# Linear attention beside a top-8 gated MLP: the reciprocal denominator spread inside DRAM, late transfers on one queue

## The chip, the cores and the metric

The kernel runs on one core of a Trainium2 chip. The metric is the time of one execution on the device, in microseconds. Five engines work side by side, each through its own list of instructions in order: TensorE (PE in the profile; its weight loads are PEld) multiplies matrices into PSUM, VectorE (DVE) and ScalarE (ACT) work on elements, GpSimd (POOL) does small work and indirect transfers, and SyncE (SP) only issues transfers. Sixteen DMA engines move the data. SyncE and ScalarE each have a queue of their own for the transfers they issue; an engine that waits for something before it issues a transfer holds back all that stands behind it in its list.

## The reference

Input x has 2048 tokens of 640 features. It is normalised (`xn`), and the output is the sum of three things: x itself, linear attention on `xn`, and a branch B on `xn`.

```
x = A_x; xn = layernorm(x)
q, k, v = split(xn @ wqkv)            # 32 heads of 20 features
phi(t) = (t + 1 if t > 0 else exp(t)) + 1e-6
kv = sum_s phi(k)_s (x) v_s;  z = sum_s phi(k)_s
den = phi(q) . z + 1e-6               # one number per token and head
A = ((phi(q) @ kv) / den) @ wo
r = xn @ w_r; idx = the 8 tokens with the largest r
y = (silu(xn[idx] @ w_gate) * (xn[idx] @ w_up)) @ w_down * sigmoid(r[idx])
out = x + A + xn + (y added to rows idx)
```

Data are bfloat16.

## The kernel before, in words

The 2048 tokens are 16 tiles of 128 partitions. First the tiles are normalised and transposed, and for each tile TensorE computes phi(k) and accumulates the Gram matrix of `xn` and phi(k), from which kv is made later. The queries are computed transposed: `pqT` holds phi(q) with features on partitions and tokens along the free axis, in 20 units (`q_mm`, L271; `q_act`, `q_phi`), five units for each block of 512 tokens.

The attention output of one tile is one product, `o_mm` (L778): `pqT` of the tile against `Ms`, which is kv times wo folded into one matrix. For that, phi(q) has to be divided by den beforehand. `den_mm` (L565) puts den into PSUM with four groups of tokens stacked on the partitions: partition 32 j + h holds head h of token group j. `den_act` (L574) makes 1/den of it with a logarithm and an exponential on ScalarE (`rden`). But `pqT` has one partition for each feature, and 20 features share a head, so each row of `rden` has to appear 20 times on other partitions. This goes through DRAM: `rden_out` or `rden_out_b` (L582, L594) writes each row 20 times from SBUF into a DRAM buffer with one row per feature (`rd`, `rd2`, `rd3`), and `rden_in` or `rden_in_b` (L588, L600) reads that into `spare`, on the partitions of `pqT`. `rden_mul` (L603) and `rden_mul_b` (L607) then multiply `pqT` by it on VectorE. It is done in three parts: tokens 0 to 1023 (offset 0, groups of 256), tokens 1024 to 1535 (offset 1024, groups of 128) and tokens 1536 to 2047 (offset 1536, groups of 128). The first part is written by one transfer of ScalarE and read by two of SyncE. The second is written by four transfers of SyncE, the third by four that ScalarE and SyncE issue in turn. Both are read back by SyncE.

Branch B picks the 8 tokens, gathers their columns, computes gate and up (`gate_up`) and `down`, and scales into `y8`. The rows that have to be changed lie in any tile. For the last five tiles (TS = 11) the kernel puts the residual rows into a DRAM copy `s_dram` (`load_s`, L112), GpSimd adds `y8` to it by an indirect transfer (L837), and the rows are read back into `x_sb` (L842). For tiles 0 to 10 another indirect transfer adds `y8` to the output in DRAM after those tiles have been stored (L849).

The last stage is the loop over t (L823): `o_mm(t)` on TensorE, `o_out(t)` (L788) adds the residual rows on VectorE and stores the tile; interleaved are `down`, the third part of 1/den (t = 0), the reload (t = 5), and the multiplies, `rden_mul` at t = 0 and 1, `rden_mul_b(t + 2)` from t = 6 to 13. Output tiles take turns in two groups of four buffers, one group for even and one for odd t. Stores of t = 0, 1, 2, 3 and of odd t are issued by ScalarE, the others by SyncE. `o_last` handles tile 15 in pieces.

The order of the instructions on every engine is the order of the code; nothing rearranges it. A framework adds the waits: for data, for buffers, and for landing counters. There are eight such counters for the transfers of SyncE and ScalarE together, used in turn; a transfer isn't issued before the last one on the same counter has landed.

Of the kernel before, what the change touches and what calls it, by code (L numbers as in the profile page):

```python
# [8 lines left out]
P = 128  # L9
S = 2048  # L10
D = 640
H = 32
DH = D // H
F = 1536
T = S // P
KC = D // P
FC = F // P
# [9 lines left out]
TS = 11  # L27
NS = TS * P

BF16 = mybir.dt.bfloat16  # L30
# [4 lines left out]
ALU = mybir.AluOpType  # L35
# [3 lines left out]
def kernel(  # L39
# [12 lines left out]
    nc = tc.nc  # L52
# [14 lines left out]
        return sm.tile(shape, dtype, tag=name, name=name)  # L67

    ps = psum.tile([P, 8, 512], F32, tag="ps", name="ps")
    rd = tc.dram_tile([4, D, 256], BF16, name="rd")  # L70
    rdb = [tc.dram_tile([D, 512], BF16, name=f"rd{tb}") for tb in (2, 3)]
    s_dram = tc.dram_tile([S - NS, D], BF16, name="s_dram")

    x_sb = big.tile([P, T, D], BF16, tag="x_sb", name="x_sb")
# [55 lines left out]
    def load_wd(lo, hi):  # L130
        SP.dma_start(wd[:, lo:hi, :], B_w_down.rearrange("(fc p) n -> p fc n", p=P)[:, lo:hi, :])
# [376 lines left out]
    load_wo()  # L508
    kcw(wu, B_w_up, 2, 3)
    kcw(wu, B_w_up, 3, KC)  # L510
    for i in range(0, FC, 4):
        load_wd(i, i + 4)
    PE.transpose(psb[0:T, 1, 0:P], r_all[:], ident[:])
    g1(T - 4)
    r_row = sb("r_row", [T, P], F32)
# [63 lines left out]
        return rden  # L579


    def rden_out(rden):  # L582
        A.dma_start(
            rd[:, :, :].rearrange("j (h i) t -> (j h) i t", i=DH),
            rden[:].unsqueeze(1).to_broadcast([P, DH, 256]),
        )

    def rden_in(j):  # L588
        SP.dma_start(
            spr[:, j * KC : (j + 2) * KC, :],  # L590
            rd[j : j + 2, :, :].rearrange("j (m p) t -> p (j m) t", p=P),
        )

    def rden_out_b(eng, i, rden, j):  # L594
        eng.dma_start(  # L595
            rdb[i][:, j * P : (j + 1) * P].rearrange("(h i) t -> h i t", i=DH),
            rden[32 * j : 32 * j + 32, :].unsqueeze(1).to_broadcast([32, DH, P]),
        )

    def rden_in_b(i):  # L600
        SP.dma_start(sprb[i], rdb[i][:, :].rearrange("(m p) t -> p m t", p=P))

    def rden_mul(j):  # L603
        sl = pqT[:, :, j * 256 : (j + 1) * 256]
        V.tensor_tensor(out=sl, in0=sl, in1=spr[:, j * KC : (j + 1) * KC, :], op=ALU.mult)

    def rden_mul_b(t):  # L607
        sl = pqT[:, :, t * P : (t + 1) * P]
        V.tensor_tensor(  # L609
            out=sl, in0=sl, in1=sprb[t // 12][:, :, t % 4 * P : (t % 4 + 1) * P], op=ALU.mult  # L610
        )

    def kv_mm(bs, bank):
# [87 lines left out]
    spr = sp_rows(0, 8, 256)  # L701
    sprb = [sp_rows(8, 12, 512), sp_rows(12, T, 512)]
# [74 lines left out]

    def o_mm(t):  # L778
        b0 = 2 * (t % 2)
# [8 lines left out]
    def o_out(t):  # L788
        b0 = 2 * (t % 2)
        o_t = evk.tile([P, 2, HW], BF16, tag=("ek", "rk")[t % 2], name=f"o{t}")  # L790
        V.tensor_tensor(  # L791
            out=o_t[:], in0=ps[:, b0 : b0 + 2, 0:HW],
            in1=x_sb[:, t, :].rearrange("p (b f) -> p b f", b=2), op=ALU.add,
        )
# [28 lines left out]
    for t in range(T - 1):  # L823
        o_mm(t)
        if t == 0:
            down()
            den_mm(1536, P, 6)
            rden3 = den_act(1536, P, 6)
            for j in range(4):
                rden_out_b((A, SP)[j % 2], 1, rden3, j)  # L830
            rden_in_b(1)
            for i in range(4):
                A.activation(  # L833
                    y8[:, i * QW : (i + 1) * QW], ps[32 * i : 32 * i + C, 5 + 2 * (i % 2), 0:QW],
                    AF.Identity, scale=gate[32 * i : 32 * i + C, 2:3],
                )
            G.indirect_dma_start(  # L837
                s_dram[:, :], bass.IndirectOffsetOnAxis(ap=idx_i[0:C, 1:2], axis=0), y8[:], None,
                bounds_check=S - NS - 1, oob_is_err=False, compute_op=ALU.add,
            )  # L840
        if t == 5:
            A.dma_start(x_sb[:, TS:T, :], s_dram[:, :].rearrange("(t p) d -> p t d", p=P))  # L842
# [39 lines left out]
```

## Time and profile before

| | |
|---|---|
| median of 3 timed runs | 114.94 us (113.46 to 117.36) |
| the profiled execution | 112.75 us |
| its span in the profile | 111.0 us |
| TensorE busy | 104.3 us |
| VectorE busy | 81.2 us |
| ScalarE busy | 58.9 us |
| GpSimd busy | 39.2 us |
| granted TensorE clock | 1.0 |

The span runs from the first to the last instruction of the profiled execution; the rest of its 112.75 us lies around it. Times within the profile are counted from the span's start. The profile shows when an instruction ran on its engine, when a transfer was issued (lines with SPq or ACTq), and, in the groups of transfers, how long it was from issue to landing.

### The profile page before, as it was taken

The numbers are of one execution on the slowest core, as the hardware profiler recorded it, in microseconds if no ns is written. First come the engines' busy times: TensorE is split into PE (matmuls) and PEld (weight loads), VectorE is DVE, ScalarE is ACT, GpSimd is POOL, SyncE is SP. The second block draws the span as 40 slices with busy tenths as digits, with TensorE's granted clock in tenths as the row PEclk, the third lists the DMA queues.
The fourth block names the chain that finished last, engine by engine and source line by source line (L and its number), as shares of the span: only waits on it lengthen the run. The fifth ranks groups of instructions, "written<-read, shape, count | busy, mean of one in ns | idle before, by whom it ended". The sixth has DMA issues, their size and how long they took to land.

```text
span 111.0 us, 2501 instructions
## 1 busy us (share of the span) xinstructions
PE 104.3 (94%) x897; PEld 61.8 (56%) x906; DVE 81.2 (73%) x186; ACT 58.9 (53%) x155; POOL 39.2 (35%) x86
## 2 busy tenths in 40 slices
PE   5899999999999999999999999999999999994990
PEld 2256645555555555564447788534457776662660
DVE  1798997789999996544349745696799766884780
ACT  1449996797877666555058352788894400000000
POOL 6903563211344448899993420000000050000040
PEclk9999999999999999999999999999999999999999
DMA  3999435792679998999999949369868199999243
GB/s 81 324 328 297 152 68 101 197 240 59 183 189 203 210 177 206 224 220 302 235 388 365 304 110 287 98 173 302 292 91 151 51 344 254 242 359 386 89 124 118
DMA packets 31655, 23.65 MB, mean 213 GB/s; under 512 B 14194, under 2 KB 30362, under 8 KB 31642
## 3 DMA queue, kind: packets, MB, share of 16 engines
q1 hardware_dynamic: 25168, 18.97, 64.3%
q10 hardware_dynamic: 6410, 4.51, 13.2%
q8 instruction: 7, 0.11, 0.5%
q14 instruction: 6, 0.05, 0.2%
q0 software_dynamic: 64, 0.01, 0.2%
HBM read 15.44 MB, written 6.08 MB: 194 GB/s over the span
## 4 chain that ended last, share of the span: by engine, by line
PE 73%; DMA 14%; ACT 3%; issue 3%; DVE 2%; ACTq 2%; SPq 0%
PE ps L274 19%; PE ps L237 19%; PE ps L266 16%; PE ps L782 5%; DMA spare<-rd 5%; DMA out_dram<-o 4%; PE ps L502 4%; DMA rd<-rden 3%; DMA x_sb<-in_A_x_dram 2%; PE ps L617 2%; PE ps L634 2%; PE ps L717 2%; PE ps L215 1%; PE ps L808 1%; ACTq L595 1%
## 5 line engine op out<-in xcount | busy, mean ns | idle before, releaser
L237 PE MATMUL ps<-wk,xnT 128*128 128x320 bf16 (+1 forms) x160 | 25.0, 300 | 0.1
L274 PE MATMUL ps<-xnT,wq 128*128 128x512 bf16 x93 | 22.9, 379 | 0.6 <-issue 0.3
L782 PE MATMUL ps<-late,pqT 128*128 128x320 bf16 x150 | 21.6, 299 | 1.4 <-DVE pqT L609 1.4
L237 PEld LDWEIGHTS <-xnT 128*128 128x128 bf16 x160 | 15.1, 98 | 8.7 <-ACT xnT L221 0.9
L266 PE MATMUL ps<-pk,xn 128*128 128x512 bf16 x78 | 19.5, 379 | 0.1
L251 ACT ACTIVATE ek<-ps 128x320 bf16<-128x320 f32 x32 | 14.8, 463 | 8.1 <-PE ps L237 8.1
L782 PEld LDWEIGHTS <-pqT 128*128 128x128 bf16 x150 | 14.1, 98 | 8.7 <-DVE pqT L609 3.1
L283 ACT ACTIVATE eq<-ps 128x512 bf16<-128x512 f32 x20 | 11.9, 597 | 9.0 <-PE ps L274 9.0
L175 DVE BATCH_NORM_STATS2 stats<-x_sb 128x6 f32<-128x320 bf16 x32 | 14.8, 474 | 2.3 <-DMA x_sb<-in_A_x_dram 2.3
L290 DVE SCALAR_TENSOR_TENSOR pqT<-eq,rq 128x512 bf16<-128x512 bf16 x20 | 13.7, 685 | 3.7 <-ACT rq L284 3.7
L259 DVE SCALAR_TENSOR_TENSOR pk<-ek,rk 128x640 bf16<-128x640 bf16 x16 | 13.0, 813 | 4.2 <-ACT rk L252 4.2
L791 DVE TENSOR_TENSOR o<-ps,x_sb 128x640 bf16<-128x640 f32 x15 | 12.3, 823 | 4.7 <-PE ps L782 3.5
L274 PEld LDWEIGHTS <-wq 128*128 128x128 bf16 x100 | 9.3, 98 | 10.7 <-issue 0.7
L252 ACT ACTIVATE rk<-ps 128x320 bf16<-128x320 f32 x32 | 14.8, 463 | 0.0
L207 POOL TENSOR_SCALAR x_sb<-x_sb,rs,nm 128x640 bf16<-128x640 bf16 x13 | 13.8, 1068 | 0.6
L266 PEld LDWEIGHTS <-xn 128*128 128x128 bf16 x80 | 7.7, 98 | 8.1
L284 ACT ACTIVATE rq<-ps 128x512 bf16<-128x512 f32 x20 | 11.9, 593 | 0.0
L186 POOL TENSOR_SCALAR t<-mv 128x1 bf16<-128x1 f32 x12 | 3.8, 316 | 21.7 <-DVE mv L177 21.4
L818 ACT CAST o<-ps 128x160 bf16<-128x160 f32 x1 | 0.3, 292 | 19.1 <-PE ps L808 19.1
L187 POOL TENSOR_TENSOR rs<-t,mhalf 128x1 f32<-128x1 bf16 x12 | 10.0, 834 | 1.0
L837 POOL DMA_INDIRECT s_dram<-y,idx_i x1 | 1.6, 1594 | 23.2 <-ACT y L833 23.2
L196 DVE TENSOR_SCALAR xn<-x_sb,mv,rs 128x640 bf16<-128x640 bf16 x16 | 7.2, 450 | 3.3 <-POOL rs L187 2.8
(123 smaller groups left out, 98.6 us busy)
## 6 DMA issues: line engine op xcount, KB each, us to landing
spare<-rd SPq DMA_DIRECT2D x4, 640.0 KB, 5.4
wg<-in_B_w_gate_dram SPq DMA_DIRECT2D x5, 384.0 KB, 3.4
wd<-in_B_w_down_dram SPq DMA_DIRECT2D x3, 640.0 KB, 13.5
out_dram<-o ACTq DMA_DIRECT2D x9, 160.0 KB, 4.0
rd<-rden ACTq DMA_DIRECT2D x1, 1280.0 KB
wu<-in_B_w_up_dram SPq DMA_DIRECT2D x3, 384.0 KB, 3.5
wo<-in_A_wo_dram SPq DMA_DIRECT2D x2, 500.0 KB, 7.7
x_sb<-in_A_x_dram SPq DMA_DIRECT2D x3, 320.0 KB, 5.8
```

What stands on the lines that cost most here:

```text
L175: V.bn_stats(out=stats[:, t, b, :], in_=x_sb[:, t, b * HW : (b + 1) * HW])
L207: G.tensor_scalar(out=x_sb[:, t, :], in0=x_sb[:, t, :], scalar1=rs1[:, sl], scalar2=nm[:, sl], op0=ALU.mult, op1=ALU.add,)
L237: PE.matmul(ps[:, b0 + b, 0:n], lhsT=xnT[:, kc, t * P : (t + 1) * P], rhs=wk[:, kc, b * HW : b * HW + n], start=(kc == 0), stop=(kc == KC ...
L251: A.activation(e[:, b, :], ps[:, b0 + b, 0:HW], AF.Exp)
L252: A.activation(r[:, b, :], ps[:, b0 + b, 0:HW], AF.Relu)
L259: V.scalar_tensor_tensor(out=pk[:, t, :].rearrange("p (b f) -> p b f", b=2), in0=e[:], scalar=1.0, in1=r[:], op0=ALU.min, op1=ALU.add,)
L266: PE.matmul(ps[:, 2 + c, :], lhsT=xn[:, t, c * P : (c + 1) * P], rhs=pk[:, t, 0:512], start=(t == 0), stop=(t == T - 1),)
L274: PE.matmul(ps[:, bank, :], lhsT=wq[:, kc, m * P : (m + 1) * P], rhs=xnT[:, kc, tb * 512 : (tb + 1) * 512], start=(kc == 0), stop=(kc == K ...
L283: A.activation(e[:], ps[:, bank, :], AF.Exp)
L290: V.scalar_tensor_tensor(out=pqT[:, m, tb * 512 : (tb + 1) * 512], in0=e[:], scalar=1.0, in1=r[:], op0=ALU.min, op1=ALU.add,)
L782: PE.matmul(ps[:, b0 + b, 0:HW], lhsT=pqT[:, kc, t * P : (t + 1) * P], rhs=Ms[:, kc, b * HW : (b + 1) * HW], start=(kc == 0), stop=(kc == ...
L791: V.tensor_tensor(out=o_t[:], in0=ps[:, b0 : b0 + 2, 0:HW], in1=x_sb[:, t, :].rearrange("p (b f) -> p b f", b=2), op=ALU.add,)
```

## The change

The three parts of 1/den take a common form, with the offset as key (`parts` gives the width of a token group):

- Out of SBUF each row goes once, not 20 times: four small transfers for a part, into `rdh`, one row per head.
- A transfer from DRAM to DRAM, `rden_copy`, repeats each row 20 times, into `rds`, one row per feature.
- One transfer reads `rds` into `spare`. For the first part that is one transfer of 1280 KB in place of two of 640 KB.

All of these transfers are issued by SyncE now. Their places in its list: the first part's copy stands where its reads stood, then the store to `s_dram`, then the read; the second part's copy stands behind its four small writes, its read behind query unit 19; the third part's copy stands behind its four small writes at t = 0, its read at t = 3. The stores of output tiles 0 to 5 are all issued by SyncE, and so is the reload of `x_sb` from `s_dram`. ScalarE keeps the stores of tiles 7, 9, 11, 13 and the last piece of tile 15. w_down is loaded in six transfers of two chunks, not three of four. No instruction that computes is added, removed or moved on its engine.

```diff
-    rd = tc.dram_tile([4, D, 256], BF16, name="rd")
-    rdb = [tc.dram_tile([D, 512], BF16, name=f"rd{tb}") for tb in (2, 3)]
+    parts = {0: 256, 1024: P, 1536: P}
+    rdh = {o: tc.dram_tile([H, 4 * w], BF16, name=f"rdh{o}") for o, w in parts.items()}
+    rds = {o: tc.dram_tile([D, 4 * w], BF16, name=f"rds{o}") for o, w in parts.items()}
...
-    for i in range(0, FC, 4):
-        load_wd(i, i + 4)
+    for i in range(0, FC, 2):
+        load_wd(i, i + 2)
...
+    def rden_out(eng, o, rden):
+        w = parts[o]
+        for j in range(4):
+            eng.dma_start(rdh[o][:, j * w : (j + 1) * w], rden[32 * j : 32 * j + 32, :])
+
+    def rden_copy(eng, o):
         eng.dma_start(
-            rdb[i][:, j * P : (j + 1) * P].rearrange("(h i) t -> h i t", i=DH),
-            rden[32 * j : 32 * j + 32, :].unsqueeze(1).to_broadcast([32, DH, P]),
-        )
+            rds[o][:, :].rearrange("(h i) t -> h i t", i=DH),
+            rdh[o][:, :].unsqueeze(1).to_broadcast([H, DH, 4 * parts[o]]),
+        )
+
+    def rden_in(eng, o):
+        eng.dma_start(spr[o], rds[o][:, :].rearrange("(m p) t -> p m t", p=P))
...
-    rden_out(den_act(0, 256, 6))
+    rden0 = den_act(0, 256, 6)
+    rden_out(SP, 0, rden0)
...
-    for j in (0, 2):
-        rden_in(j)
+    rden_copy(SP, 0)
     load_s(TS, T)
+    rden_in(SP, 0)
...
-    for j in range(4):
-        rden_out_b(SP, 0, rden2, j)
+    rden_out(SP, 1024, rden2)
+    rden_copy(SP, 1024)
...
-    rden_in_b(0)
+    rden_in(SP, 1024)
...
-        eng = nc.sync if t % 2 == 0 and t > 2 else nc.scalar
+        eng = nc.sync if t % 2 == 0 or t < 6 else nc.scalar
...
-            for j in range(4):
-                rden_out_b((A, SP)[j % 2], 1, rden3, j)
-            rden_in_b(1)
+            rden_out(SP, 1536, rden3)
+            rden_copy(SP, 1536)
...
+        if t == 3:
+            rden_in(SP, 1536)
         if t == 5:
-            A.dma_start(x_sb[:, TS:T, :], s_dram[:, :].rearrange("(t p) d -> p t d", p=P))
+            SP.dma_start(x_sb[:, TS:T, :], s_dram[:, :].rearrange("(t p) d -> p t d", p=P))
```

More of the change, by code (lines that the diff above doesn't have):

```diff
@@ L579, in den_act @@
         return rden
[L582 to L585, printed above, removed]
[L586 to L601 removed]
+    def rden_out(eng, o, rden):
[3 more added lines that the diff above has]
+    def rden_copy(eng, o):
+        eng.dma_start(
+            rds[o][:, :].rearrange("(h i) t -> h i t", i=DH),
+            rdh[o][:, :].unsqueeze(1).to_broadcast([H, DH, 4 * parts[o]]),
+        )
+    def rden_in(eng, o):
+        eng.dma_start(spr[o], rds[o][:, :].rearrange("(m p) t -> p m t", p=P))
     def rden_mul(j):
         sl = pqT[:, :, j * 256 : (j + 1) * 256]
[L605 removed]
+        V.tensor_tensor(out=sl, in0=sl, in1=spr[0][:, :, j * 256 : (j + 1) * 256], op=ALU.mult)
     def rden_mul_b(t):
@@ L609, in rden_mul_b @@
         V.tensor_tensor(
-            out=sl, in0=sl, in1=sprb[t // 12][:, :, t % 4 * P : (t % 4 + 1) * P], op=ALU.mult
+            out=sl, in0=sl, in1=spr[t // 4 * 512][:, :, t % 4 * P : (t % 4 + 1) * P], op=ALU.mult
         )
@@ L699, in sp_rows @@
         return spare[:, a:b, :].rearrange("p a b -> p (a b)").rearrange("p (r f) -> p r f", f=w)
-    spr = sp_rows(0, 8, 256)
-    sprb = [sp_rows(8, 12, 512), sp_rows(12, T, 512)]
+    spr = {o: sp_rows(o // P, o // P + w // 32, 4 * w) for o, w in parts.items()}
     Ms = late[:, 0:KC, :]
-    for j in (0, 2):
-        rden_in(j)
+    rden_copy(SP, 0)
     load_s(TS, T)
+    rden_in(SP, 0)
     A.copy(GT[:, 0:4, 512:D], ps[:, 2, :].rearrange("p (c f) -> p c f", c=4))
```

## The prediction

> **What bounds the kernel now.** I read the page's head first, then its share of the chain that ended last.
>
> ```profile
> span 111.0 us, 2501 instructions
> PE 104.3 (94%) x897; PEld 61.8 (56%) x906; DVE 81.2 (73%) x186; ACT 58.9 (53%) x155; POOL 39.2 (35%) x86
> ...
> PE 73%; DMA 14%; ACT 3%; issue 3%; DVE 2%; ACTq 2%; SPq 0%
> ```
>
> TensorE is busy for 94% of the span, so a change that touches only transfers can gain little: the gaps that a transfer causes. The table of waits and the chain in order of time show where such a gap is.
>
> ```profile
> PE ps L782 <- DVE pqT L609: 1.4, 1, 1.4
> ```
>
> ```profile
> 86.71 0.74 ACTq L595
> ...
> 88.33 4.73 DMA out_dram<-o
> 93.06 0.02 issue
> 93.08 3.19 DMA rd<-rden
> ...
> 96.33 5.34 DMA spare<-rd
> 101.66 0.02 issue
> 101.69 0.50 DVE pqT L609
> 102.19 0.05 issue
> 102.24 2.89 PE ps L782 x20
> ...
> 108.15 0.29 ACT o L818
> ```
>
> The last quarter hangs on 1/den of tokens 1536 to 2047 (block 3): written to DRAM, read back into `spare` at 101.66, multiplied into `pqT` by VectorE, used by TensorE at 102.24. The output store of 88.33 stands in this chain although its data have nothing to do with 1/den. In the program every DMA takes one of eight landing counters in turn, and an issue waits until the DMA eight places before it has landed; the fourth write of 1/den stood eight behind that store. TensorE idles 1.4 us, once. That is the most that the change can win inside the span.
>
> VectorE sets when each thing is needed. Columns: start, duration, engine, line, operation, tiles, and in brackets idle time and its releaser.
>
> ```profile
> 81.00 0.82 DVE L605 TENSOR_TENSOR pqT<-pqT,spare 128x1280 bf16<-128x1280 bf16 x1
> ...
> 94.31 0.48 DVE L609 TENSOR_TENSOR pqT<-pqT,spare 128x640 bf16<-128x640 bf16 x1
> 95.09 0.82 DVE L791 TENSOR_TENSOR o<-ps,x_sb 128x640 bf16<-128x640 f32 x1 [0.29 <-PE ps L782]
> ...
> 96.48 0.83 DVE L791 TENSOR_TENSOR o<-ps,x_sb 128x640 bf16<-128x640 f32 x1 [0.17 <-issue]
> ...
> 99.39 0.82 DVE L791 TENSOR_TENSOR o<-ps,x_sb 128x640 bf16<-128x640 f32 x1 [0.17 <-issue]
> 101.69 0.49 DVE L609 TENSOR_TENSOR pqT<-pqT,spare 128x640 bf16<-128x640 bf16 x1 [1.48 <-DMA spare<-rd]
> 102.10 0.82 DVE L791 TENSOR_TENSOR o<-ps,x_sb 128x640 bf16<-128x640 f32 x1
> 102.83 0.48 DVE L609 TENSOR_TENSOR pqT<-pqT,spare 128x640 bf16<-128x640 bf16 x1
> ```
>
> So the first part of 1/den is due at 81.0, block 2 at 94.3, block 3 at 100.2 (end of the output add of 99.39, token tile 10). The add of tile 8 (96.48) reuses the buffer of tile 0, so tile 0 must have been stored by then. The add of tile 11 (102.10) needs the rows of `x_sb` that are reloaded from `s_dram`.
>
> **The change part by part.** The times at which 1/den is ready, and the issues of SyncE now (first start, sum of the group):
>
> ```profile
> 63.91 0.42 ACT L578 ACTIVATE rden<-ld 128x256 bf16<-128x256 f32 x1
> ...
> 79.91 0.31 ACT L578 ACTIVATE rden<-ld 128x128 bf16<-128x128 f32 x1
> ...
> 85.71 0.31 ACT L578 ACTIVATE rden<-ld 128x128 bf16<-128x128 f32 x1
> ...
> 87.50 0.38 ACT L833 ACTIVATE y<-ps,gate 8x160 bf16<-8x160 f32 x1 [1.48 <-issue]
> ...
> 93.63 0.39 ACTq L842 DMA_DIRECT2D x_sb<-s_dram  x1
> ```
>
> ```profile
> 49.55 5.97 SPq L131 DMA_DIRECT2D wd<-in_B_w_down_dram  x3
> 71.75 1.16 SPq L589 DMA_DIRECT2D spare<-rd  x2
> 73.02 1.79 SPq L113 DMA_DIRECT2D s_dram<-x_sb  x1
> 80.24 3.16 SPq L595 DMA_DIRECT2D rd<-rden  x4
> 86.12 0.37 SPq L601 DMA_DIRECT2D spare<-rd  x1
> ```
>
> Prices of transfers come from landings (issue to landing: writes of L595, 160 KB each; reads into `spare`, 640 KB; the reload; the smallest store) and from what the DMA engines moved in three stretches (last number, GB/s): reads in 512-byte pieces, writes in 256-byte pieces, long pieces.
>
> ```profile
> DMA to landing us min/median/max: 2.9/3.5/5.5
> ```
>
> ```profile
> DMA to landing us min/median/max: 4.5/5.4/6.3
> ```
>
> ```profile
> x_sb<-s_dram ACTq DMA_DIRECT2D x1, 800.0 KB, 5.4
> ...
> out_dram<-o ACTq DMA_DIRECT2D x1, 80.0 KB, 1.6
> ```
>
> ```profile
> 74.00:77.00 3.00, 3.00 (x16) 1.37 (x15) 2.53 (x5) 2.51 (x6) 0.00 (x0) 1.00 1.17 317
> 82.00:85.00 3.00, 3.00 (x81) 2.16 (x79) 2.97 (x5) 1.75 (x4) 0.00 (x0) 1.00 1.02 170
> 98.00:102.00 4.00, 2.81 (x20) 1.59 (x18) 2.36 (x4) 0.00 (x0) 0.00 (x0) 1.00 1.07 382
> ```
>
> A write: 2.9 less 164 KB at 170 GB/s (1.0) leaves 1.9 us fixed. A read: 4.5 less 655 KB at 317 (2.1) leaves 2.4 fixed. At 382 GB/s, 640 KB (655,360 bytes) take 1.7 us, 1280 KB 3.4, the 800 KB reload 2.1, one 160 KB store 0.43. A read back of 640 KB then takes 2.4 + 1.7 = 4.1; of 1280 KB 5.8. Four small writes, 64 KB or less together, take the 1.6 of the smallest store after the last issue, at 0.37 an issue (row of 86.12).
>
> *The copy inside DRAM* is an operation that the trace does not show. If a byte costs what it costs between DRAM and SBUF, 640 KB take 1.9 + 1.7 = 3.6 and 1280 KB 5.3. If reading and writing share the 382 GB/s, because both ends are DRAM, the data count twice: 5.3 and 8.8. If they share the 317 of the shorter pieces, 6.0 and 10.2. I take the middle one: no stretch above shows more than 382 with reads and writes together, and here every byte is both. Both other ends stay for the range.
>
> The Trainium skill, page "DMA: Bandwidth & Descriptors", section "Latency and other measured facts", gives 214 GB/s per direction for large copies between HBM tensors; by that figure 640 KB would take an estimated 1.9 + 3.1 = 5.0 and the sum below would be 0.6 us lower; no row here shows such a copy.
>
> *First part (tokens 0 to 1023).* Out at 64.36, last of four issues at 65.5, landed 67.1; copy landed 67.1 + 8.8 = 75.9. The 800 KB to `s_dram` now go behind the copy in the queue and end at about 77.6, where the read's data begin anyway; the read back lands 75.9 + 5.8 = 81.7. It is due at 81.0: 0.7 late, where before it was on time. VectorE is full there (2.97 of 3.00 in the stretch 82 to 85), so the rest of the projections moves with it, until a later wait swallows this. By the cheap copy it lands at 78.2, with 2.8 in hand.
>
> *Block 2.* Ready at 80.22; last issue 81.35; landed 82.95; copy 82.95 + 5.3 = 88.25; read 92.35, due 94.3: hidden, with 2 us in hand.
>
> *Block 3.* Ready at 86.03, but SyncE waits for block 2's copy: its four writes start at 88.6, end at 89.7, and lie behind block 2's read in SyncE's one queue, so they land at 92.4. Copy 92.4 + 5.3 = 97.7. Behind the copy in the queue stand the stores of tiles 0, 1, 2, which ScalarE used to issue (88.33 in the chain is one of them): they land at 98.1, 98.6, 99.0. The add of tile 8 waits for the first: 98.1 instead of 96.48, 1.6 late. The read back, issued at 97.7, lands at 101.8; it is due 3.7 after the add of tile 8 (100.2 less 96.48), also at 101.8. Hence the wait removed (1.4) is replaced by one of 1.6 at tile 8.
>
> *The reload of `x_sb`* moves from ScalarE's queue (93.63) to SyncE's, behind that read and the stores of tiles 3 and 4: issued at 98.9, its data start when the read's end (101.4) and two stores are through (0.9), take 2.1, and land about 0.4 after: 104.8. The add of tile 11 waits for it: 104.8 instead of 102.10. Behind it, 0.4 is caught up: the products of tile 13 could begin at 102.83 + 0.48 = 103.31, but began after those of tile 12, at 102.24 + 1.45 (half of the 2.89 for twenty) = 103.69; with the old stall gone, tile 12's are done long before. Sum: 2.7 - 0.4 = +2.3 us.
>
> The Trainium skill, same page, section "Issuing engines are not separate DMA queues", says that issuing on several engines saves only the issuer's time. By this rule the reload would land an estimated 5.4 after its issue, at 104.3, half a microsecond sooner; the chain's SyncE writes waiting behind a ScalarE store speak against leaving the order of issue out.
>
> *ScalarE* loses the two issues of L595 and most stores: the values `y` start at about 86.1 instead of 87.50, and so does the scatter into `s_dram`. That gains nothing, since the reload then waits in SyncE's queue. The issue of 64.36 was followed by a wait for TensorE.
>
> *w_down in six pieces*: SyncE ended its three issues at 55.5 and is not needed before 64.36; three more issues of 0.37 and their waits are covered by these 8.8 us, and the products that use w_down begin late:
>
> ```profile
> 83.92 1.01 PE L727 MATMUL ps<-wd,late 128*32 128x160 bf16 x48
> ```
>
> Nothing, either way; without that cover, 1.1 us.
>
> *A buffer.* In the changed build, tile 9 takes the buffer of tile 7, no longer that of tile 1. Tile 7's add ends at 95.91 (row of 95.09) and its store is issued then, still by ScalarE; at the fastest landing (1.6) it has landed by 97.6, just ahead of the add of tile 9 at 98.00. Up to 0.5 us, inside the 1.6 already counted.
>
> **How it stands to the median.** The profiled execution took 112.75 (1.75 around its span); the runs shown have 114.94. I add the difference to the median: 114.94 + 2.3 = 117.2, 2.0% more. About 2%, or 2.3 us, is what a measurement of this kernel can tell from none.
>
> **The rivals.**
>
> *The copy costs one way only; not slower.* Block 2's copy lands at 86.55, its read at 90.65; block 3's writes 90.7, copy 94.3, stores from 94.7 (no wait at tile 8), read 98.4 (due 100.2, the old stall is gone), reload 101.4 against 100.8. The end comes 102.10 - 101.4 + 0.4 = 1.1 earlier: 113.8. It decides by the copy's landing time: below about 4.2 us for 640 KB the end is not later than before. For it: the engines move each byte once. Against: a DRAM row on both sides. Chance 0.21.
>
> *The stall goes and no new one comes*, if the reload too lands by 100.8: 1.4 earlier, 113.5. Timed runs lie up to 4.6 us above the profiled one; if part of that is this same DMA chain, the gain may exceed 2.3 us. Chance 0.11.
>
> *The copy is dearer still* (6.0 and 10.2): the first read lands at 83.1, 2.1 us late under a full VectorE; copy of block 3 at 99.1, tile 8 at 99.5, reload 106.2, end 106.2 - 102.10 - 0.4 = 3.7 later: 118.6. Chance 0.26.
>
> *The reload doesn't become the bound* (it overtakes the stores or shares the engines with the read): then tile 8's 1.6 remains against the 1.4 won, about 115.1; it lies between the cases and is counted within the first two.
>
> **How the numbers follow.** The middle copy has 0.42 and gives 117.2, its own range 115.5 to 118.3. Slower by over 2%: all of the dear copy (0.26) and half of the middle one (0.21), 0.47. Faster by over 2%: 0.11. Rest: 0.42. The range from 113.3 to 119.6 takes in the cheap and the dear copy with their spread.
>
> **What would show it.** In the changed profile: three rows `rds<-rdh` whose landing gives the copy's price directly (5.3 at 640 KB, 8.8 at 1280); SyncE waiting on `rds` or `rdh` landings between 82 and 98; an idle time of VectorE before the multiply of 81.0 ended by a DMA into `spare`; a DMA wait `out_dram<-o` ahead of the add of tile 8; and, in place of `spare<-rd` at 101.69, `x_sb<-s_dram` ahead of tile 11. The prediction is wrong if the copy of 640 KB lands in under 4.2 us, or if the reload isn't the last thing TensorE's tail waits for.

## The result and the profile after

The changed kernel took 122.38 us (median of 6 runs, 121.49 to 124.35) beside 114.20 us (112.99 to 117.36) of the kernel before on the same chip: a ratio of 1.078, 95% interval 1.070 to 1.085. The forecast was 117.2 us with a range up to 119.6, so the change cost three and a half times what was forecast (8.2 us for 2.3). Here and below, medians are over all runs of a kernel, while ratios and their intervals compare the faster runs of each, and the profiled execution of the changed kernel, 123.97 us, is not one of those. Its mean granted TensorE clock is 0.958; the other runs have 0.954 to 0.986.

The head of the page of the changed kernel:

```profile
span 122.2 us, 2514 instructions
PE 108.8 (89%) x906; PEld 63.7 (52%) x906; DVE 81.4 (67%) x186; ACT 58.8 (48%) x155; POOL 39.8 (33%) x86
...
PE 51%; DMA 33%; DVE 6%; issue 3%; SPq 2%; ACT 2%; POOL 1%; DVEq 0%; POOLq 0%; ACTq 0%
```

The span grew by 11.2 us. TensorE has the same products and yet is busy 4.5 us longer, and transfers hold 33% of the chain that ended last, where they held 14%. The end of that chain in order of time (start, duration, step):

```profile
65.95 2.75 DMA rdh<-rden
68.85 8.82 DMA rds<-rdh
77.75 6.62 DMA spare<-rds
84.39 0.84 DVE pqT L600
...
95.81 5.23 DMA out_dram<-o
...
103.63 6.80 DMA out_dram<-o
...
111.77 5.53 PE ps L777 x20
```

The first three are the new route of the first part: small writes, copy, read back, each issued when the one before has landed, 18.4 us in all. The store at 95.81 is that of tile 0; it stands in SyncE's list behind block 3's copy. What was held up is on VectorE (start, duration, engine, line, operation, tiles; in brackets idle time and its releaser):

```profile
84.39 0.83 DVE L600 TENSOR_TENSOR pqT<-pqT,spare 128x1280 bf16<-128x1280 bf16 x1 [3.04 <-DMA spare<-rds]
...
101.16 0.82 DVE L786 TENSOR_TENSOR o<-ps,x_sb 128x640 bf16<-128x640 f32 x1 [0.49 <-DMA out_dram<-o]
...
105.24 0.49 DVE L604 TENSOR_TENSOR pqT<-pqT,spare 128x640 bf16<-128x640 bf16 x1 [0.35 <-DMA spare<-rds]
110.48 0.82 DVE L786 TENSOR_TENSOR o<-ps,x_sb 128x640 bf16<-128x640 f32 x1 [4.75 <-DMA out_dram<-o]
```

The first part's multiply starts at 84.39 where it started at 81.00. The add of tile 8 starts at 101.16 (96.48 before), the add of tile 11 at 110.48 (102.10). For that last wait both views name a store, the one issued at 103.63. But a landing leaves sixteen marks in the trace, one for each DMA engine, and by the last of them that store landed at 110.89, after the add had begun. The reload of `x_sb` landed at 110.29, 0.2 us ahead of the add, which needs the reloaded rows. In the traces of the two filler experiments below, with the same list, the view names the reload.

SyncE's issues (start, sum of the group) show where the time before these landings went:

```profile
80.52 1.71 SPq L587 DMA_DIRECT2D rdh<-rden  x4
85.11 0.53 SPq L590 DMA_DIRECT2D rds<-rdh  x1
89.67 0.38 SPq L596 DMA_DIRECT2D spare<-rds  x1
90.16 2.14 SPq L587 DMA_DIRECT2D rdh<-rden  x4
95.23 0.53 SPq L590 DMA_DIRECT2D rds<-rdh  x1
95.81 1.63 SPq L791 DMA_DIRECT2D out_dram<-o  x3
100.68 0.38 SPq L596 DMA_DIRECT2D spare<-rds  x1
...
102.22 0.51 SPq L838 DMA_DIRECT2D x_sb<-s_dram  x1
```

From 85 to 101 SyncE is held three times until a landing: block 2's read waits for its copy (issued 4.6 us before), block 3's copy for its small writes (5.1 after the first of them), block 3's read for its copy (5.4). Between 95.81 + 1.63 and 100.68 it issues nothing, although `x_sb` could be reloaded from 95.34 on, when the scatter into `s_dram` had landed; the reload starts at 102.22, 8.6 us later than before.

The TensorE clock is the second thing that is new. Rows of 1 us each; the third number from the end is the granted clock:

```profile
86.00:87.00 1.00, 1.00 (x10) 0.43 (x12) 1.00 (x2) 0.00 (x0) 0.00 (x0) 0.74 0.36 117
...
89.00:90.00 1.00, 1.00 (x16) 0.51 (x5) 0.22 (x1) 0.62 (x3) 0.00 (x0) 0.56 0.02 7
...
110.00:111.00 1.00, 0.00 (x0) 0.00 (x0) 0.52 (x1) 0.00 (x0) 0.00 (x0) 0.68 0.23 81
...
117.00:118.00 1.00, 1.00 (x10) 0.72 (x8) 0.69 (x1) 0.00 (x0) 0.00 (x0) 0.90 0.00 0
```

and TensorE's groups at these places (in brackets the gap before):

```profile
85.27 1.72 PE L777 MATMUL ps<-late,pqT 128*128 128x320 bf16 x10 [2.37 <-DVE pqT L600]
86.92 1.79 PE L722 MATMUL ps<-wd,late 128*32 128x160 bf16 x48
...
111.77 5.51 PE L777 MATMUL ps<-late,pqT 128*128 128x320 bf16 x20 [4.44 <-DVE pqT L604]
```

The rows between those shown have 0.50. So behind a gap of 2.37 us the clock is 0.5 for 3.4 us (86.5 to 89.9: 0.74 over a microsecond means that 0.52 of it ran at half), and around the end of one of 4.44 us for 6.8 us (110.4 to 117.2). The 48 products of `down` take 1.79 us instead of 1.01, and twenty products of the output 5.51 instead of 2.89.

### The profile page after: what moved, and what is told of

Its sections match the earlier page's. It is cut to its first block, busy times and chain, and to the rows that moved or that the text cites. A ratio compares the mean times of both kernels' runs of the same rounds, so it can differ in the third digit from the quotient of the medians.

```text
span 122.2 us, 2514 instructions
## 1 busy us (share of the span) xinstructions
PE 108.8 (89%) x906; PEld 63.7 (52%) x906; DVE 81.4 (67%) x186; ACT 58.8 (48%) x155; POOL 39.8 (33%) x86
## 4 chain that ended last, share of the span: by engine, by line
PE 51%; DMA 33%; DVE 6%; issue 3%; SPq 2%; ACT 2%; POOL 1%; DVEq 0%; POOLq 0%; ACTq 0%
PE ps L239 14%; PE ps L268 13%; PE ps L777 12%; DMA out_dram<-o 10%; DMA rds<-rdh 7%; PE ps L276 6%; DMA spare<-rds 5%; DMA wk<-in_A_wqkv_dram 4%; DMA xnT<-xn 4%; DMA rdh<-rden 2%; PE ps L504 2%; PE ps L722 1%; DVE stats L177 1%; DVE xn L198 1%; SPq L97 1%
## 5 line engine op out<-in xcount | busy, mean ns | idle before, releaser
L777 PE MATMUL ps<-late,pqT 128*128 128x320 bf16 x150 | 24.7, 326 | 7.5 <-DVE pqT L604 5.1
L777 PEld LDWEIGHTS <-pqT 128*128 128x128 bf16 x150 | 15.1, 105 | 16.7 <-DVE pqT L604 6.6
L276 PE MATMUL ps<-xnT,wq 128*128 128x512 bf16 x100 | 23.7, 379 | 0.0
```

Of the source, the lines that this page charges most:

```text
L276: PE.matmul(ps[:, bank, :], lhsT=wq[:, kc, m * P : (m + 1) * P], rhs=xnT[:, kc, tb * 512 : (tb + 1) * 512], start=(kc == 0), stop=(kc == K ...
L777: PE.matmul(ps[:, b0 + b, 0:HW], lhsT=pqT[:, kc, t * P : (t + 1) * P], rhs=Ms[:, kc, b * HW : (b + 1) * HW], start=(kc == 0), stop=(kc == ...
```

## The experiments

Four theories were tried: that the copy itself is dear, that the chain of landings in SyncE's one list is the cost, that the reload's place in that list is, and that the lower clock is.

**The reload by ScalarE.**

```diff
-            SP.dma_start(x_sb[:, TS:T, :], ...)
+            A.dma_start(x_sb[:, TS:T, :], ...)
```

> The changed kernel with one edit: ScalarE, not SyncE, issues the reload of x_sb from s_dram. Theory 'the reload stands too late in SyncE's queue': the wait of 4.75 us before the add of tile 11 goes, and with it the long gap on TensorE; the store of tile 0 now shares a landing counter with the reload and may wait for it, which gives about 1.5 us back; time about 118 (116 to 119.5), ratio to before 1.02 to 1.045. Rival 'the add of tile 11 only waits because everything behind block 3's copy is late': the reload landing earlier moves the wait to the multiply of tile 12 and the time stays above 121.

Measured: 121.22 us (120.95 to 121.54), ratio 1.070 [1.062, 1.078]. VectorE's wait moved from tile 11 to tile 8:

```profile
103.86 0.82 DVE L786 TENSOR_TENSOR o<-ps,x_sb 128x640 bf16<-128x640 f32 x1 [5.20 <-DMA out_dram<-o]
```

The reload was issued at 94.70 and landed at 101.83. But the store of tile 0 takes the same landing counter, so SyncE issued it at 101.91, and the block-3 read behind it at 103.30. The wait was not taken away, only put on another tile: a miss by 3 us, near the rival's time, and the first sign that the list and the counters, not one transfer, decide.

**Without the copy, everything else as changed.** Each row is written 20 times from SBUF, by SyncE.

```diff
-            eng.dma_start(rdh[o][:, j * w : (j + 1) * w], rden[32 * j : 32 * j + 32, :])
+            eng.dma_start(
+                rds[o][:, j * w : (j + 1) * w].rearrange("(h i) t -> h i t", i=DH),
+                rden[32 * j : 32 * j + 32, :].unsqueeze(1).to_broadcast([32, DH, w]),
+            )
...
-        eng.dma_start(rds[o] ..., rdh[o] ...)
+        pass
```

> The changed kernel without the copy inside DRAM: each row is written 20 times from SBUF straight into the buffer with one row per feature, as in the kernel before, but by SyncE; all other issues stand as in the changed kernel. Theory 'the copy's own round trip is the cost': the first part lands before 81, block 3's read about 97 to 99, no long wait is left; time 112.5 to 115, ratio 0.985 to 1.01. Rival 'putting all late issues into SyncE's one queue is the cost': it stays at 118 or more, ratio over 1.03, with the wait for the reload before tile 11 still there.

Measured: 119.70 us (118.33 to 120.06), ratio 1.056 [1.047, 1.066], and on VectorE:

```profile
81.17 0.82 DVE L599 TENSOR_TENSOR pqT<-pqT,spare 128x1280 bf16<-128x1280 bf16 x1 [0.25 <-DMA spare<-rds]
...
105.86 0.83 DVE L785 TENSOR_TENSOR o<-ps,x_sb 128x640 bf16<-128x640 f32 x1 [5.17 <-DMA x_sb<-s_dram]
```

Without any copy the first part is on time and block 3's read lands at 97.8, but most of the loss stays: the reload, issued at 99.15 behind that read, lands at 105.67. The rival's forecast (118 or more) held. In this list, the copy is not the larger part.

**The copy, most other parts undone.** w_down in three pieces, the first small writes and the early stores by ScalarE, block 3's read at t = 0 and the reload by ScalarE. Block 3's four small writes stay with SyncE, where the kernel before let ScalarE issue two.

```diff
-    for i in range(0, FC, 2):
-        load_wd(i, i + 2)
+    for i in range(0, FC, 4):
+        load_wd(i, i + 4)
...
-    rden_out(SP, 0, rden0)
+    rden_out(A, 0, rden0)
...
-        eng = nc.sync if t % 2 == 0 or t < 6 else nc.scalar
+        eng = nc.sync if t % 2 == 0 and t > 2 else nc.scalar
...
+            rden_in(SP, 1536)
...
-        if t == 3:
-            rden_in(SP, 1536)
...
-            SP.dma_start(x_sb[:, TS:T, :], ...)
+            A.dma_start(x_sb[:, TS:T, :], ...)
```

> The copy inside DRAM, with the other parts of the change undone: w_down in three pieces, stores of tiles 0 to 3 and of odd tiles and the reload issued by ScalarE, the first part's four small writes by ScalarE, block 3's read right behind its copy. Theory 'the copy costs by itself': the first part still lands near 83 to 84 against 81 due, TensorE waits some 2 us and the granted clock drops for 3.4 us after it; the long wait at tile 11 is gone; time 116.5 to 119, ratio 1.02 to 1.045. Rival 'one queue is the cost': within 1% of before.

Measured: 122.22 us (121.29 to 124.61), ratio 1.071 [1.063, 1.080]; slower than expected by 3 us.

```profile
109.08 0.49 DVE L604 TENSOR_TENSOR pqT<-pqT,spare 128x640 bf16<-128x640 bf16 x1 [5.27 <-DMA spare<-rds]
```

Here block 3's third and fourth small writes were issued at 96.06 and 96.82, after waits for output stores on the same counters; copy and read came behind them, to 109.05. The copy adds one more landing to a chain that was late already (the 1.48 us before tile 13 in the kernel before). But this run doesn't price the copy alone. The four small writes of the first part, now in ScalarE's list, hold it for 3.40 us from 64.49 on, so that TensorE waits 1.19 us for ScalarE before 69.56 and its clock is 0.5 from 71.1 to 74.5; a product that starts at 78.70 in the changed kernel starts at 81.71 here. How much of the 7.1% is this and how much the copy was not separated; the copy in a good order, below, is the cleaner price.

**Filler products in the gaps.** 11 and 20 products that nobody uses, of 0.236 us each (measured), ahead of tiles 0 and 13.

```diff
+        if t == 0:
+            warm(11, 7)
+        if t == 13:
+            warm(20, 7)
```

> The changed kernel with 11 extra matmuls of 128x512 on zeros ahead of tile 0's product and 20 ahead of tile 13's, so that TensorE is busy while it waits (2.4 us and 4.3 us at 0.216 us each). Theory 'a gap on TensorE also costs the clock behind it': the granted clock stays at 1.0 through the output stage, the products of w_down take 1.0 us again and not 1.8, and the time falls by 1 to 3 us to 119.5 to 121.5. Rival 'the lower clock in the records is a state of the chip': the clock still drops and the time stays at 122 to 123.

Measured: 122.43 us (121.71 to 122.94), ratio 1.078 [1.067, 1.090], mean clock 1.000: the clock as the theory had it, the time as the rival.

```profile
86.86 1.01 PE L722 MATMUL ps<-wd,late 128*32 128x160 bf16 x48
...
108.78 4.48 PE L148 MATMUL ps<-zw 128*128 128x512 bf16 x19
113.10 2.88 PE L777 MATMUL ps<-late,pqT 128*128 128x320 bf16 x20
```

With the gaps filled the clock stays at 1 and all products take their old time: the gaps were the reason for the lower clock. But the filler ended at 113.26 and tile 13 started at 113.10, some 1.3 us after its data, which gave the gain back. The size of the clock's share stayed open, and a shorter filler was run later.

**The first part as before** (written by ScalarE 20 times from SBUF, read in two transfers), blocks 2 and 3 through the copy.

```diff
-    rden_out(SP, 0, rden0)
+    A.dma_start(
+        rd[:, :, :].rearrange("j (h i) t -> (j h) i t", i=DH),
+        rden0[:].unsqueeze(1).to_broadcast([P, DH, 256]),
+    )
...
-    rden_copy(SP, 0)
+    for j in (0, 2):
+        SP.dma_start(spr[0][:, j * KC : (j + 2) * KC, :], rd[j : j + 2, :, :] ...)
...
-    rden_in(SP, 0)
```

> The changed kernel with the first part (tokens 0 to 1023) as in the kernel before: one transfer of ScalarE writes each row 20 times, two transfers of SyncE read back, the store to s_dram behind them. Parts two and three go by the copy. Theory 'the first part's lateness is its own cost': the idle 3.0 us of VectorE at 81 and the 2.4 us of TensorE go, the small writes of block 2 land near 83 and not 85, and the wait before the add of tile 11 stays at 4 to 6 us; time 118 to 120.5, ratio 1.035 to 1.055. Rival 'the end hangs on SyncE's chain alone, the first gap is hidden': time within 1% of the changed kernel, 121.5 to 123.

Measured: 121.37 us (120.31 to 122.48), ratio 1.077 [1.059, 1.094]. The time is above the 120.5 expected at most. The 3 us wait ahead of the first part is gone, and the end hardly moves:

```profile
104.02 0.49 DVE L605 TENSOR_TENSOR pqT<-pqT,spare 128x640 bf16<-128x640 bf16 x1 [1.44 <-DMA spare<-rds]
...
108.21 0.82 DVE L794 TENSOR_TENSOR o<-ps,x_sb 128x640 bf16<-128x640 f32 x1 [3.69 <-DMA x_sb<-s_dram]
```

The reload, issued at 99.82, again takes 8.2 us. The lateness of the first part is swallowed by the wait at the end.

**The reload ahead of block 3's read**, both by SyncE.

```diff
         if t == 3:
-            rden_in(SP, 1536)
-        if t == 5:
             SP.dma_start(x_sb[:, TS:T, :], ...)
+            rden_in(SP, 1536)
```

> The changed kernel with SyncE issuing the reload of x_sb two places earlier in its list, ahead of block 3's read and behind the store of tile 2, in the time in which SyncE waits for block 3's copy (issue near 97.5, not 102.2). Theory 'the place in SyncE's list is the cost of the reload, not SyncE': the reload lands near 104 to 105, block 3's read a little later, 106 to 107; the wait before tile 11 falls from 4.75 us to under 1, the one before the multiply of tile 12 grows to 1 to 2; time 117.5 to 119.5, ratio 1.03 to 1.045. Rival 'DMA engines or landing counters keep it late anyway': above 121.

Measured: 120.22 us (118.45 to 122.06) beside 114.39 us of the kernel before, between the theory's range and the rival's. The reload landed at 103.47, and tile 11 no longer waits. Tile 9 does:

```profile
105.64 0.83 DVE L786 TENSOR_TENSOR o<-ps,x_sb 128x640 bf16<-128x640 f32 x1 [3.68 <-DMA out_dram<-o]
```

It reuses the buffer of tile 7, whose store ScalarE issued at 100.19 and which landed at 105.52, behind the reload and the read. About 2 us gained, by the medians, and a new wait found.

**No copy, the reload ahead, and all stores but the last piece by SyncE**: the second and the sixth experiment together, with

```diff
-        eng = nc.sync if t % 2 == 0 or t < 6 else nc.scalar
+        eng = nc.sync
```

> No copy inside DRAM (rows written 20 times from SBUF by SyncE), the reload ahead of block 3's read, and all output stores but the last piece issued by SyncE, so that every late transfer is in one queue in an order in which no issue waits for a younger store. Theory 'order in the list, not one queue, made the last experiment with direct writes slow': reload and block 3's read both land by 99, no long wait is left, and the old 1.4 us gap is gone too; time 112 to 114, ratio 0.98 to 1.0. Rival 'one queue is too slow for these transfers': over 116, with a wait for a store or for block 3's read above 2 us.

Measured: 112.89 us (111.72 to 115.2), ratio 0.994 [0.988, 1.001]. One queue and one issuing engine are no handicap if the order is right: the time can't be told from that of the kernel before, and the ratio is 6.2 points below the second experiment's. What separates the two is the reload's place and who issues the stores.

```profile
102.73 0.49 DVE L603 TENSOR_TENSOR pqT<-pqT,spare 128x640 bf16<-128x640 bf16 x1 [2.34 <-DMA spare<-rds]
```

That wait is all that is left; block 3's read now lands behind the reload's data.

The Trainium skill, page "DMA: Bandwidth & Descriptors", section "Issuing engines are not separate DMA queues", says that transfers of all issuing engines run on the same DMA engines, and that issuing on several of them saves only the time of issue. This run agrees as far as bandwidth goes: SyncE alone issues nearly everything, at no loss. The waits in an issuer's list are a matter apart: the second experiment makes the same transfers, with ScalarE issuing a few of the stores, and its list costs the 6.2 points.

**The price of the transfers by themselves.** This kernel computes nothing of the reference; it runs transfers one after the other, each issued when the last has landed, two rounds of each size.

> Only transfers, each waiting for the landing of the one before, on an otherwise idle chip: 640 rows of 2 KB, then of 1 KB, twice: SBUF to DRAM; DRAM to DRAM row by row; 32 rows DRAM to DRAM; DRAM to DRAM with each of 32 rows read 20 times; DRAM to SBUF; SBUF to DRAM with each row 20 times. The kernel computes nothing of the reference. One-way price: a copy lands as fast as a store, 5.0 to 5.5 us at 1280 KB and 3.5 to 4 at 640. Two-way price, as in the prediction: 8.8 and 5.3. 'Reading one row 20 times is slow': the copy row by row at the one-way price and only the spreading one at 8.8 and 5.0.

The DMA issues of this run (tiles, count, KB each, median us to landing; `spread<-rows` writes each row 20 times from DRAM, `spread<-back` from SBUF, `copy<-plain` copies row by row inside DRAM):

```profile
copy<-plain SPq DMA_DIRECT2D x2, 1280.0 KB, 6.0
spread<-rows SPq DMA_DIRECT2D x2, 1280.0 KB, 7.0
back<-spread SPq DMA_DIRECT2D x2, 1280.0 KB, 6.2
spread<-back SPq DMA_DIRECT2D x2, 1280.0 KB, 8.1
...
copy<-plain SPq DMA_DIRECT2D x2, 640.0 KB, 4.4
spread<-rows SPq DMA_DIRECT2D x2, 640.0 KB, 4.1
back<-spread SPq DMA_DIRECT2D x2, 640.0 KB, 4.3
spread<-back SPq DMA_DIRECT2D x2, 640.0 KB, 4.9
...
rows<-copy SPq DMA_DIRECT2D x2, 64.0 KB, 2.1
```

A copy inside DRAM costs about what a read into SBUF costs, so its two ends do not add up: 6.0 and 4.4 are far below the two-way price for 1280 KB (8.8) and below that for 640 KB (5.3), though also above the one-way price expected. And the new route is not cheaper than the old even alone: a small transfer of 32 rows (here inside DRAM, in the kernel out of SBUF) and the spread take 2.1 + 7.0 = 9.1 us for 1280 KB where the direct spread takes 8.1, and 2.1 + 4.1 = 6.2 for 640 KB where it takes 4.9.

**The copy in the good order.** The changed kernel with the reload ahead of the read and the stores by SyncE (the two diffs above).

> The changed kernel with the route through two DRAM tiles kept, and only SyncE's list put in the order of the fast version: the reload of x_sb stands ahead of block 3's read, and all output stores but the last piece are issued by SyncE. Theory (the order of the list costs the most, the copy itself little): the first part's read still lands about 2.5 to 3 us late and VectorE waits there (the copy is kept), tile 8 still waits up to 2 us for the store of tile 0 behind block 3's copy, but tile 9 doesn't wait for tile 7 and the add of tile 11 not for the reload. 116 to 118 us, ratio 1.015 to 1.035. Rival (the copy is what costs, whatever the order): 119 or more, with a wait of 3 us or more for 1/den at tile 12.

Measured: 116.85 us (116.43 to 117.26), ratio 1.030 [1.026, 1.035]. Time and waits as the theory had them, with one of 1.64 us for block 3's rows besides:

```profile
84.45 0.82 DVE L600 TENSOR_TENSOR pqT<-pqT,spare 128x1280 bf16<-128x1280 bf16 x1 [3.30 <-DMA spare<-rds]
...
100.72 0.82 DVE L786 TENSOR_TENSOR o<-ps,x_sb 128x640 bf16<-128x640 f32 x1 [1.51 <-DMA out_dram<-o]
...
106.09 0.49 DVE L604 TENSOR_TENSOR pqT<-pqT,spare 128x640 bf16<-128x640 bf16 x1 [1.64 <-DMA spare<-rds]
```

The order, with SyncE issuing the stores, takes the ratio from 1.078 to 1.030; the copy, in a good order, costs the 3.6 points between 0.994 and 1.030.

**The same, with the first part as before.** The diffs of the fifth and the last experiment together.

> The same, and the first part of 1/den written and read as in the kernel before, so that only blocks 2 and 3 go through the copy. Theory: the wait of VectorE ahead of the first part's multiply and the TensorE gap behind it are gone, and with them the granted clock of 0.5 after that gap; 114 to 116.5 us, 1.5 to 2.5 us less than with the copy in the first part. Rival (the first part's lateness is swallowed by a later wait, as when only the first part was undone in the changed order): less than 1 us between the two.

Measured: 115.99 us (115.71 to 116.33), ratio 1.023 [1.019, 1.027]: 0.9 us less, not the 1.5 to 2.5 expected, so the rival holds. Most of the copy's cost lies in blocks 2 and 3; tile 8 now waits 2.62 us where it waited 1.51.

**Block 3's read first, the reload in two pieces**, otherwise the version without the copy in its good order.

```diff
         if t == 3:
-            SP.dma_start(x_sb[:, TS:T, :], ...)
             rden_in(SP, 1536)
+            for a, b in ((TS, 13), (13, T)):
+                SP.dma_start(x_sb[:, a:b, :], s_dram[a * P - NS : b * P - NS, :] ...)
```

> The version without the copy and with the ordered list, but with block 3's read of 1/den first and the reload behind it in two transfers, for token tiles 11 and 12 and for 13 to 15. Theory: the 2.3 us that VectorE waited there for block 3's rows (read landed 102.71) go, because the read lands at about 98 to 100, and the first piece of the reload (320 KB) lands by 101.5, before tile 11 needs it: 111.5 to 113 us, ratio 0.98 to 0.99. Rival: the second piece or the store of tile 0 becomes the wait, and the time stays at 113 to 115, ratio 0.99 to 1.00.

Measured: 112.21 us (111.98 to 112.71), ratio 0.992 [0.989, 0.995].

```profile
101.31 0.82 DVE L785 TENSOR_TENSOR o<-ps,x_sb 128x640 bf16<-128x640 f32 x1 [0.69 <-DMA out_dram<-o]
```

The read landed at 98.40 and the waits for 1/den and for the reload are gone; 0.69 us for a store remain. This version beats both kernels, the one before by 0.8%, or 0.9 us: a little less than the gap of 1.4 us that it closes.

**w_down in six pieces in the kernel before.**

```diff
-    for i in range(0, FC, 4):
-        load_wd(i, i + 4)
+    for i in range(0, FC, 2):
+        load_wd(i, i + 2)
```

> The kernel before with w_down loaded in six pieces instead of three, nothing else changed. Theory: no effect on the time, since the products that use w_down begin 20 us later: ratio 0.995 to 1.005. Rival: three more places among the eight landing counters shift which issue waits for which landing later, and the time moves by over 1% in either direction.

Measured: 113.78 us (median of 12 runs), ratio 1.001 [0.998, 1.004]. No effect.

**A shorter filler in the changed kernel**: 11 and 12 products.

```diff
+        if t == 0:
+            warm(11, 7)
+        if t == 13:
+            warm(12, 7)
```

> The changed kernel with filler products in its two TensorE gaps as before, but 12 instead of 20 in the second, so that they end (12 by 0.236 us behind 108.8: about 111.6) before tile 13's weights are ready and delay nothing. Theory: what the lower granted clock costs is the difference to the changed kernel: tile 13's and 14's products take 2.9 us instead of the 5.5 of its profile, the first gap's share being swallowed by the later wait; 1 to 2.6 us less, 119.8 to 121.4, ratio 1.055 to 1.07. Rival (the clock costs nothing here, since the tail behind it hangs on stores): 122 to 122.8, ratio 1.07 to 1.08.

Measured: 120.58 us (119.19 to 122.28), ratio 1.058 [1.052, 1.065]. On TensorE and on VectorE:

```profile
109.71 2.75 PE L148 MATMUL ps<-zw 128*128 128x512 bf16 x11
112.67 2.89 PE L777 MATMUL ps<-late,pqT 128*128 128x320 bf16 x20 [0.21 <-DVE pqT L604]
```

```profile
111.39 0.82 DVE L786 TENSOR_TENSOR o<-ps,x_sb 128x640 bf16<-128x640 f32 x1 [3.11 <-DMA x_sb<-s_dram]
```

Now the filler ends before the data come, the twenty products from tile 13 on take 2.89 us, and the time falls although the kernel does more: by 1.9% by the ratios, whose intervals don't overlap, and by 0.8 us (7.4 instead of 8.2) by the medians over the kernel before on the same chip. So the clock's share is 1 to 2 us of 8.2; the wait for the reload is as long as before.

**The stores by SyncE, the reload where the change put it.**

```diff
-        eng = nc.sync if t % 2 == 0 or t < 6 else nc.scalar
+        eng = nc.sync
```

> The changed kernel with all output stores but the last piece issued by SyncE and nothing else changed: the reload of x_sb stays behind block 3's read. This is the other half of the order edit: the reload ahead alone gave 120.2, both together 116.85. Theory (the two belong together: the stores matter only where tile 9 would wait for one by ScalarE): no gain, as the reload, with a store more ahead of it in the list, lands at 110 to 111 as before; 121.5 to 123.5, ratio 1.07 to 1.085. Rival (ScalarE's stores cost by themselves, wherever the reload stands): 119.5 or less.

Measured: 121.41 us (119.46 to 122.1), ratio 1.063 [1.054, 1.073]. The median is just under the theory's range, and one of the four runs reached the rival's 119.5.

```profile
109.97 0.82 DVE L786 TENSOR_TENSOR o<-ps,x_sb 128x640 bf16<-128x640 f32 x1 [3.64 <-DMA x_sb<-s_dram]
```

The reload lands at 109.85, as late as ever. Over the kernel before on the same chip, by the medians, the changed kernel stands at +8.2 us, the stores alone at +8.2, the reload ahead alone at +5.8, both at +3.5. By the ratios the stores alone gain 1.4 points (1.078 to 1.063), with intervals that overlap a little. So with the reload behind, the stores are worth little, and whether it is nothing was not settled; with the reload ahead, a store is the next wait, as the trace of that run showed.

## Why the prediction was wrong

**The sign was the likelier one, the size was not.** Slower by over 2% had the largest chance, 0.47, but the whole range ended 2.8 us below the result, and the dearest rival (118.6) 3.8 below. Against its own profile, the forecast was 112.75 + 2.3 = 115.05; the profiled execution took 123.97, that is 8.9 more (by the medians the change cost 8.2 for 2.3, 5.9 more). Landing by landing:

| step of the prediction | forecast | measured |
|---|---|---|
| first part: small writes landed | 67.1 | 68.7 |
| its copy, issue to landing | 8.8 | 8.82 |
| its read landed | 81.7 | 84.36 |
| block 2: small writes landed | 82.95 | 85.03 |
| its read landed | 92.35 | 94.25 |
| block 3: small writes landed | 92.4 | 95.16 |
| its copy landed | 97.7 | 100.66 |
| its read landed | 101.8 | 105.22 |
| reload issued | 98.9 | 102.22 |
| reload landed | 104.8 | 110.29 |
| from the add of tile 11 to the last cast, against before | -0.4 | +2.25 |

**What bounds the kernel now** was read rightly: the only gap that the change could close was the 1.4 us before tile 13, and the version that closes it wins 0.8%.

**The step that failed is the reload of `x_sb`, a mis-sized term.** Place and mechanism were as forecast: the reload is the last thing that the tail waits for. "2.7 later" was 8.4 (110.48 less 102.10). Of the 5.5 us that its landing lay beyond the forecast, 3.3 are a later issue and 2.2 a longer way. The later issue is a sum of small terms along SyncE's chain. The fourth small write of the first part took 1.69 us to issue, its read 6.62 us instead of 5.8; block 2's small writes lie behind that read, as I had seen for block 3's but not for them; each lateness is handed on, since each step waits for a landing. The longer way: by the step's own rule, counted from the read's landing at 105.22, the reload would have landed at 108.2. The first of the sixteen DMA engines was done at 108.52, the last at 110.29. A landing is that of the slowest engine, and no term had room for that. It is no accident of one execution: with the same list, in the first filler run, the reload was issued at 102.36 and landed at 110.33.

**The sign of the tail was wrong.** I let 0.4 us be caught up behind the add of tile 11; in truth 2.25 were lost, since the new gap of 4.44 us brought a granted clock of 0.5. The kernel before has no such stretch at its end, and the prediction had no term for it. The two filler runs show the cause: with the clock at 1, the second took 5.79 us from the add of tile 11 to the last cast, beside 6.05 before and 8.30 in the changed kernel, so that 0.26 was caught up, not far from the 0.4. They put the clock's share at 1 to 2 us of the usual time; between the forecast and this profiled execution it is 2.65. The remaining 0.8 of the 8.9 us lie between reload and add (0.2) and behind the last cast (0.6).

**The copy inside DRAM**: the size I took (8.8 and 5.3) was close to what the kernel showed (8.82, 4.5 and 5.4), but not for my reason. Alone, a plain copy takes 6.0 and 4.4, which speaks against two ends sharing the 382 GB/s; the spread copy takes 7.0 and 4.1. (The estimate of 5.0 for 640 KB, from the 214 GB/s of the Trainium skill's page "DMA: Bandwidth & Descriptors", section "Latency and other measured facts", is above what the copy takes alone and between the two in the kernel.) The extra in the kernel goes with engines shared with other transfers and with straggling ones (the first part's copy: first engine done 6.7 us after its issue, last 8.8); neither was tested by itself, and what makes an engine straggle stays open. The rival "the copy costs one way only" was thus nearer in mechanism, and its conclusion, not slower, still false: it let everything hang on the copy's price, and without any copy the list as changed costs 5.6%.

**First part**: 0.7 late was forecast, 3.04 us of waiting came; that a later wait swallows it held for the most part (0.9 us between the two ordered copy versions; no difference that can be told in the changed order). **Block 2**: hidden, as forecast; no wait at its multiply. **Block 3**: the wait at tile 8 for the store of tile 0 is there, but of 0.49 us only; the add comes 4.7 us later than before instead of 1.6, and tile 7's was 4.4 late already (99.45 for 95.09). **ScalarE**: the values `y` did not come earlier but later, at 89.96 instead of 87.50, with TensorE's first gap; nothing hung on it. **w_down**: nothing, as forecast (ratio 1.001). **A buffer**: no wait at tile 9 in the changed kernel, but 3.68 us as soon as the reload stands ahead; my bound of 0.5 took a store's landing at its fastest, 1.6 us, and behind two large transfers it took 5.3.

The removed gap alone would have been worth about 0.8%, and it did not go: block 3's rows came at 105.22, where they came at 101.66.

## What to carry to other kernels

Read an issuing engine's list as a chain of landings: a transfer that waits for another's landing blocks everything behind it, so independent transfers (a reload, stores) belong ahead of such a wait, and a route in two hops costs one more landing for each hop even if it moves fewer bytes out of SBUF. When adding up such a chain, price each landing behind what is still in the queue and by its slowest DMA engine, and leave room for the lower clock that can follow a TensorE gap. Before a transfer is moved, look at whose buffer and whose landing counter waits for it.

## What the runs showed of the hardware that was not expected

The granted clock falls in fixed stretches: 3.4 us at 0.5 after the gap of 2.37, 6.8 us after that of 4.44. Their starts keep a beat too: 86.5 and 110.4 lie 23.9 us apart, seven times 3.41, and the two of the third experiment, 71.1 and 108.7, lie 37.6 apart, eleven times. The same kind of gap does not always do it. One of 2.31 us left the clock at 1 (first experiment, before 84.78), another of 2.31 was followed by 3.4 us at 0.5 (first part as before in the good order, 100.6 to 104.0). Gaps of 2.63 us (copy in the good order) and 2.97 us (stores by SyncE) left it at 1:

```profile
85.34 1.53 PE L777 MATMUL ps<-late,pqT 128*128 128x320 bf16 x10 [2.63 <-DVE pqT L600]
86.80 1.01 PE L722 MATMUL ps<-wd,late 128*32 128x160 bf16 x48
```

The Trainium skill, page "TensorE: Matmul & The Clock Gate", section "Part 1: The HAM clock gate", describes a window of 3.4 us that runs freely and sets the clock to half after an idle one. The stretches of 3.4 and 6.8 us agree, and so does the chance in whether a gap is punished; that a gap of 2.37 us was enough does not agree with a whole window of idleness, and the measured gap decides.

Within one transfer the sixteen DMA engines can finish 2 us apart and more: 77.67 against 75.57 for the first part's copy, 110.29 against 108.52 for the reload, 101.00 against 97.95 for the reload of the version without the copy in its good order. A copy inside DRAM of 1280 KB lands after 6.0 us alone, close to a read into SBUF of that size (6.2).
